# Attention and expert in units of 384 tokens, with other loads, load order and tile sets

## The chip, the cores and the metric

The kernel runs on one core of a Trainium2 chip, in one launch. The metric is the device time of the program in microseconds (us). A core has five engines that each run their own instructions in order: PE (TensorE, matmuls), DVE (VectorE), ACT (ScalarE), POOL (GpSimd) and SP (SyncE, which here only issues DMAs). They meet through semaphores. Matmuls write to PSUM, a small memory of eight banks per partition; a tile in it is free again when its readers are done.

## The reference

```python
# q, k, v: (4, 8, 768, 64) float32;  w_in: (512, 2048);  w_out: (2048, 512)
k_sum = k.reshape(B, H, nb, 32, D).max(axis=3)       # nb = 24 blocks of 32 tokens
v_sum = v.reshape(B, H, nb, 32, D).mean(axis=3)
scores_l = scale * q @ k.T, kept where |i - j| < 16, else -1e9
scores_s = scale * q @ k_sum.T + log(32)
a = softmax(concat(scores_l, scores_s))
x = a @ concat(v, v_sum)                             # then (tokens 3072, 512)
h = x @ w_in
out = (h * sigmoid(1.702 * h)) @ w_out               # (3072, 512) float32
```

A window attention with 24 block summaries beside the window feeds a two-layer expert whose activation is the quick form of gelu.

## The kernel before, in words

The work goes by batch: four batches of 768 tokens, 8 heads in 4 pairs p. For a batch the kernel loads q, k and v in float32, casts them to bf16, and turns each pair of k and q into the layout [head dimension, token] by transposes on PE (`tk`, line 237, and `tq`, line 266). From the transposed tile `ps_t` in PSUM, DVE copies k into `kx`: 12 tiles of 128 columns, each holding 64 tokens, the 24 block maxima and the 16 tokens on either side. `qz` holds q with zeros beside each head, so that one matmul makes the scores of both heads of a pair.

`vw` holds v in the same 12 tiles of rows, with a column of ones for the row sums. Its summary rows and its neighbours' rows are on other partitions than where they were made, so they are moved by six DMAs from SBUF to SBUF at the end of `vsum` (line 214): two of `vw<-vs` (the block sums) and four of `vw<-vw` (the halos). The matmuls of `values` read `vw` and wait for these six.

`scores` (276) makes 4 score tiles with one exponential on ACT and one multiplication by the mask on DVE; `values` (291) multiplies with `vw`, takes the reciprocal of the row sums and scales on DVE; `tx` (313) transposes the result into `xT`. `ff_in` (318) is the first layer with the gelu on ACT, written to `gT`; `ff_out` (328) the second, whose result ACT copies from `po` to `osb` and SP stores.

Every engine runs in the order in which the program is written: the class `_Ordered` records each instruction of `pe`, `dve`, `act`, `pool` and `sp` with that order (so all of them have line L27 in the profile). The order around the change is this. SP issues the loads of batch 0 (line 102), then, in `load_batch(1)`, those of batch 1, and then, in `vsum`, the six DMAs of `vw`. POOL issues the weights (`load_weights`, line 179, eight DMAs that also cast to bf16) after its casts of v. Attention of batch 0 then runs alone, as the list `att` says. From there the loop over batches (371) runs all of `ff_in` of batch b with the transposes of batch b+1 among them (the list `todo`), then all of `ff_out` of batch b with one piece of the attention of batch b+1 behind every four matmuls.

A load of q or k is one DMA for a head, with rows of 64 numbers (256 bytes): partition p takes tokens p, 128+p and so on. `kx`, `qz`, `vw` and `gT` exist once; the float32 tiles twice (`stage`, two buffers). PSUM has three buffers `sc` (transposes, scores, block sums), one `av` of two banks (values) and three `mm` (both expert layers).

Of the kernel before, what the change touches and what calls it, by code (L numbers as in the profile page):

```python
# [34 lines left out]
def kernel(  # L35
# [23 lines left out]
    HALF = S // 2  # L59

# [17 lines left out]
    def load_qk(b, p, which):  # L78
        src = q if which == "q" else k
        t = stage.tile([128, NJ, 2, D], F32, name=f"{which}f{p}", tag=f"{which}f{p}")  # L80
        for hh in range(2):
            sp.dma_start(out=t[:, :, hh, :],
                         in_=src[b, 2 * p + hh].rearrange("(j p) d -> p j d", p=128))
        return t

    def load_v(b):
        t = stage.tile([128, NJ, H, D], F32, name="vf", tag="vf")
        for hh in range(H):
            sp.dma_start(out=t[:, :, hh, :],
                         in_=v[b, hh].rearrange("(j p) d -> p j d", p=128))  # L90
        return t
# [3 lines left out]
    def load_batch(b):  # L95
        for p in range(NP):
            raw[b, "k", p] = load_qk(b, p, "k")
            raw[b, "q", p] = load_qk(b, p, "q")
            if p == 0:
                raw[b, "v"] = load_v(b)  # L100

    load_batch(0)


# [25 lines left out]
    for par, own, blk, halo in ((0, 0, 64, 96), (1, 64, 0, 32)):  # L130
        m = mk[:, par, :]
        nc.gpsimd.memset(m, 1.0)
        sel(mk[own:own + 64, par, :], window - 1, -1, 1)
        sel(mk[own:own + 64, par, :], window - 1, 1, -1)
        sel(mk[blk:blk + 32, par, :], nb - 1, 0, -1)
        hm = mk[halo:halo + 32, par, :]

        sel(hm, -(QT - 16 - (window - 1)), 1, -1)
        sel(hm, -16, 0, 1)
        lf = left[halo:halo + 32, :]  # L140

        nc.gpsimd.memset(lf, 1.0)
        sel(lf, window - 1 - 16, -1, 1)
        sel(lf, 15, 0, -1)
    for par, halo in ((0, 96), (1, 32)):
        sl = slice(halo, halo + 32)
        for t in range(2 + par, NQ, 2):
            nc.gpsimd.tensor_copy(out=mk[:, t, :], in_=mk[:, par, :])
        for t in range(par, NQ, 2):
            if t == NQ - 1:  # L150
                nc.gpsimd.tensor_copy(out=mk[sl, t, :], in_=left[sl, :])
            elif t > 0:
                nc.gpsimd.tensor_add(mk[sl, t, :], mk[sl, t, :], left[sl, :])


    kx, qz, xT = [], [], []
    for p in range(NP):
        kt = keep.tile([128, NQ, 128], BF16, name=f"kx{p}")
        k4 = kt.rearrange("p (j e) c -> p j e c", e=2)
        nc.vector.memset(k4[:, :, 0, 88:96], 0.0)  # L160
        nc.vector.memset(k4[:, :, 1, 24:32], 0.0)
        nc.vector.memset(kt[:, 0, 96:112], 0.0)
        nc.vector.memset(kt[:, NQ - 1, 48:64], 0.0)
        kx.append(kt)
        qt = keep.tile([128, NQ, 2, QT], BF16, name=f"qz{p}")
        nc.vector.memset(qt[0:64, :, 1, :], 0.0)
        nc.vector.memset(qt[64:128, :, 0, :], 0.0)
        qz.append(qt)
        xT.append(keep.tile([128, S], BF16, name=f"xT{p}"))
# [201 lines left out]
    for b in range(B):  # L371
# [23 lines left out]
        while todo:  # L395
            todo.pop(0)()
# [36 lines left out]
```

## Time and profile before

| | |
|---|---|
| times of 3 runs, us | 315.4, 315.85, 461.52 |
| median, us | 315.85 |
| the profiled execution: its time, us | 314.48 |
| its span from the first to the last instruction, us | 312.4 |
| busy in the span: PE, DVE, ACT, POOL, us | 222.7, 130.5, 121.1, 59.2 |
| mean granted TensorE clock | 0.861 |
| bytes moved by DMA, MB | 32.33, of it 27.88 on SP's queue |

The page of the profile gives, engine by engine, the busy share of the span in 40 equal slices of 7.8 us (one digit each, in tenths; 9 is 90% or more), with the granted TensorE clock and the load of the 16 DMA engines below. The chain of waits follows the work that ended last back to the start, each row with its start, its length and what it is. The groups list the instructions of one kind with count, busy time and the mean of one in ns, and the idle time of the engine before them with what ended it. "SPq" is SP's queue of DMA instructions. `po<-w_out_sb,gT` reads: the tile po is written from w_out_sb and gT.

### The profile page before, as it was taken

What the parts mean: (1) busy time and instruction counts of PE and PEld (TensorE: products, weight loads), DVE (VectorE), ACT (ScalarE), POOL (GpSimd) and SP (SyncE); (2) the same over time, 40 slices, a digit from 0 to 9 for tenths busy, and PEclk for the clock granted to TensorE, in tenths of its full rate; (3) what the DMA queues carried; (4) which work ended last, traced back from release to release, by engine and by line L of the source; (5) the groups of instructions that cost most, each with busy time, mean ns of one, the idle gap of its engine ahead of it and who ended that gap; (6) DMA issues with size and microseconds to landing.
All of it is one profiled execution on the core that took longest, in us unless ns stands there. A gap on an engine that the chain in (4) does not pass through costs nothing.

```text
span 312.4 us, 4176 instructions
## 1 busy us (share of the span) xinstructions
PE 222.7 (71%) x1578; PEld 135.5 (43%) x1592; DVE 130.5 (42%) x306; ACT 121.1 (39%) x218; POOL 59.2 (19%) x126
## 2 busy tenths in 40 slices
PE   1230000003565899999989999999999999999995
PEld 0110000003454466555556665555665555565442
DVE  6220010005887267366627736662872666100000
ACT  1340110000223365743366574327657342777111
POOL 7691000002002940000195000029200000000000
PEclk9985555555555699999999999999999999999999
DMA  9999999999990003111169981010040111100121
GB/s 172 217 197 195 195 196 224 219 201 214 210 200 0 0 3 61 28 52 51 67 149 207 220 154 69 34 67 36 0 85 4 69 48 53 37 0 2 47 87 67
DMA packets 85875, 32.33 MB, mean 103 GB/s; under 512 B 76128, under 2 KB 82784, under 8 KB 85856
## 3 DMA queue, kind: packets, MB, share of 16 engines
q1 hardware_dynamic: 81632, 27.88, 44.3%
q0 software_dynamic: 4224, 4.19, 8.0%
q8 instruction: 12, 0.20, 0.3%
q14 instruction: 7, 0.06, 0.1%
HBM read 27.26 MB, written 6.29 MB: 107 GB/s over the span
## 4 chain that ended last, share of the span: by engine, by line
PE 64%; SPq 21%; DVE 11%; issue 2%; DMA 1%; ACT 0%; ACTq 0%
PE ph L27 27%; PE po L27 25%; SPq L27 21%; DVE x_sb L27 5%; PE ps_t L27 4%; PE ps_av L27 4%; PE ps_s L27 3%; PE ps_vs L27 1%; DVE xT L27 1%; DVE kx L27 1%; DVE rc L27 1%; DVE qz L27 1%; DMA vw<-vw 1%; DVE a_sb L27 1%; DVE ks L27 1%
## 5 line engine op out<-in xcount | busy, mean ns | idle before, releaser
L27 PE MATMUL po<-w_out_sb,gT 128*128 128x512 bf16 x370 | 92.6, 379 | 0.7
L27 PE MATMUL ph<-xT,w_in_sb 128*128 128x384 bf16 x512 | 90.0, 329 | 0.5 <-DVE xT L27 0.5
L27 ACT ACTIVATE gT<-ph 128x384 bf16<-128x384 f32 x128 | 62.9, 491 | 38.1 <-PE ph L27 37.6
L27 PEld LDWEIGHTS <-w_in_sb 128*128 128x128 bf16 x512 | 49.3, 99 | 31.6 <-issue 2.5
L27 PE MATMUL ps_av<-vw,a_sb 128*128 128x130 bf16 x192 | 19.0, 243 | 57.0 <-DMA vw<-vw 53.6
L27 ACT ACTIVATE a_sb<-ps_s 128x512 bf16<-128x512 f32 x48 | 27.7, 595 | 80.8 <-PE ps_s L27 80.7
L27 PEld LDWEIGHTS <-gT 128*128 128x128 bf16 x384 | 34.6, 98 | 28.6
L27 POOL CAST vw<-vf 128x512 bf16<-128x512 f32 x42 | 24.0, 613 | 101.9 <-DMA out_dram<-osb 74.3
L27 PEld LDWEIGHTS <-a_sb 128*128 128x128 bf16 x192 | 15.2, 108 | 63.8 <-issue 53.7
L27 DVE TENSOR_TENSOR a_sb<-a_sb,mk 128x512 bf16<-128x512 bf16 x48 | 20.2, 425 | 45.4 <-ACT a_sb L27 45.0
L27 DVE TENSOR_TENSOR x_sb<-ps_av,rc 64x384 bf16<-64x384 f32 x64 | 35.5, 555 | 1.5
L27 ACT ACTIVATE osb<-po 128x512 f32<-128x512 f32 x24 | 14.3, 597 | 38.5 <-PE po L27 25.1
L27 PE MATMUL ps_s<-qz,kx 128*128 128x128 bf16 x192 | 20.1, 238 | 10.0 <-DVE qz L27 9.8
L27 DVE COPY kx<-ps_t 128x768 bf16<-128x768 bf16 (+2 forms) x48 | 15.2, 345 | 25.6 <-PE ps_t L27 25.5
L27 DVE RECIPROCAL rc<-ps_av 128x12 f32<-128x12 f32 x32 | 7.4, 231 | 41.9 <-PE ps_av L27 41.8
L27 PEld LDWEIGHTS <-kx 128*128 128x128 bf16 x192 | 15.8, 108 | 20.0 <-DVE qz L27 10.6
L27 POOL CAST kb<-kf 128x768 bf16<-128x768 f32 x12 | 9.9, 827 | 55.0 <-PE ps_t L27 54.2
L27 DVE COPY qz<-ps_t 64x768 bf16<-64x768 bf16 x32 | 17.6, 551 | 0.9 <-PE ps_t L27 0.7
L27 DVE TENSOR_REDUCE ks<-ps_t 128x24 bf16<-128x768 bf16 x16 | 15.2, 947 | 0.0
L27 PE MATMUL ps_t<-ident,x_sb 128*128 128x128 bf16 x96 | 10.6, 242 | 4.8 <-DVE x_sb L27 4.8
L27 PE MATMUL ps_t<-ident,kb 128*128 128x128 bf16 x96 | 9.3, 242 | 6.2 <-DVE kb L27 6.2
L27 ACT ACT_TABLE_LOAD x8 | 10.3, 1283 | 6.8 <-DMA qf<-in_q_dram 6.7
(40 smaller groups left out, 100.4 us busy)
## 6 DMA issues: line engine op xcount, KB each, us to landing
kf<-in_k_dram SPq DMA_DIRECT2D x32, 192.0 KB, 4.4
qf<-in_q_dram SPq DMA_DIRECT2D x32, 192.0 KB, 4.5
vf<-in_v_dram SPq DMA_DIRECT2D x32, 192.0 KB, 4.4
out_dram<-osb SPq DMA_DIRECT2D x24, 256.0 KB, 2.0
w_in_sb<-in_moe_w_in_dram POOLq DMA_DIRECT2D x4, 512.0 KB, 11.1
w_out_sb<-in_moe_w_out_dram POOLq DMA_DIRECT2D x4, 512.0 KB, 21.6
vw<-vs SPq DMA_DIRECT2D x8, 148.5 KB
vw<-vw SPq DMA_DIRECT2D x8, 99.0 KB, 3.9
```

The source lines that it names most:

```text
L27: r = f(*a, **kw)
```

## The change

The unit of the expert and of the attention is half a batch, 384 tokens: eight units u, with batch u // 2 and half u % 2. In a unit `ff_in` runs 16 groups of 4 matmuls, and `ff_out` 12 steps (3 tiles of 128 tokens by 4 parts), and beside the 12 steps stands the attention of the next unit, by the table `plan`. `scores` now makes 6 tiles in one go (one exponential and one mask multiplication of 768 columns). The k of a whole batch and its v are prepared in the `ff_in` of the unit with half 1 of the batch before, q half by half: `tq` for the second half in the `ff_in` of half 0, for the next batch's first half in that of half 1.

q and k are loaded with three consecutive tokens on a partition, a run of 768 bytes, two heads and 384 tokens to a DMA; v still in runs of 256 bytes, with 128 tokens of all heads to a DMA. Since the tokens now lie three to a partition, the transposes are plain matmuls with the identity as the moving side, float32 in PSUM, and each writes every third column (`p3[:, r]`). DVE therefore reads k and q in float32 from PSUM.

The order of the loads on SP is k of pairs 0 and 1, v, k of pairs 2 and 3, the first halves of q of pairs 0 and 1, the six DMAs of `vw`, the other q of batch 0, and then batch 1. POOL issues the weights behind its casts: the first chunk of `w_in` after the second cast of q, the other seven after the fourth.

`kx`, `vw` and `gT` exist twice (by batch or unit, even and odd), `qz` once for each half of a batch; the float32 tiles once. PSUM has two buffers `big` of two banks each (k and q transposes, scores, values), one `x` (block sums and `tx`), and three `mm` as before.

The core of the diff:

```diff
-    stage = ctx.enter_context(tc.tile_pool(name="stage", bufs=2))
+    stage = ctx.enter_context(tc.tile_pool(name="stage", bufs=1))
     castp = ctx.enter_context(tc.tile_pool(name="cast", bufs=3))
-    attp = ctx.enter_context(tc.tile_pool(name="att", bufs=2))
+    attp = ctx.enter_context(tc.tile_pool(name="att", bufs=4))
     outp = ctx.enter_context(tc.tile_pool(name="outp", bufs=3))
-    psc = ctx.enter_context(tc.tile_pool(name="psc", bufs=3, space=bass.MemoryType.PSUM))
-    pav = ctx.enter_context(tc.tile_pool(name="pav", bufs=1, space=bass.MemoryType.PSUM))
+    psb = ctx.enter_context(tc.tile_pool(name="psb", bufs=2, space=bass.MemoryType.PSUM))
+    psx = ctx.enter_context(tc.tile_pool(name="psx", bufs=1, space=bass.MemoryType.PSUM))
...
-    def load_qk(b, p, which):
-        src = q if which == "q" else k
-        t = stage.tile([128, NJ, 2, D], F32, name=f"{which}f{p}", tag=f"{which}f{p}")
-        for hh in range(2):
-            sp.dma_start(out=t[:, :, hh, :],
-                         in_=src[b, 2 * p + hh].rearrange("(j p) d -> p j d", p=128))
-        return t
+    def load_k(b, p):
+        t = stage.tile([128, 2, 2, JH, D], F32, name=f"kf{p}", tag=f"kf{p}")
+        for half in range(2):
+            sp.dma_start(out=t[:, half].rearrange("p h r d -> p h (r d)"),
+                         in_=k[b, 2 * p:2 * p + 2, half * HALF:(half + 1) * HALF]
+                         .rearrange("h (p r) d -> p h (r d)", r=JH))
+        raw["k", p] = t
...
+    def load_q(b, p, half):
+        t = stage.tile([128, 2, JH, D], F32, name=f"qf{p}{half}", tag=f"qf{p}{half}")
+        sp.dma_start(out=t.rearrange("p h r d -> p h (r d)"),
+                     in_=q[b, 2 * p:2 * p + 2, half * HALF:(half + 1) * HALF]
+                     .rearrange("h (p r) d -> p h (r d)", r=JH))
+        raw["q", p, half] = t
...
+    def load_v(b):
+        for c in range(3):
+            t = stage.tile([128, H, 2, D], F32, name=f"vf{c}", tag=f"vf{c}")
+            for j in range(2):
+                r0 = (2 * c + j) * 128
+                sp.dma_start(out=t[:, :, j, :],
+                             in_=v[b, :, r0:r0 + 128].rearrange("h p d -> p h d"))
+            raw["v", c] = t
...
+    kx = [[keep.tile([128, NQ, 128], BF16, name=f"kx{p}_{s}") for s in range(2)]
+          for p in range(NP)]
+    qz = [[keep.tile([128, TH, 2, QT], BF16, name=f"qz{p}_{s}") for s in range(2)]
+          for p in range(NP)]
+    vw = [keep.tile([128, NQ, H, VC], BF16, name=f"vw{s}") for s in range(2)]
+    vs = keep.tile([128, H, VC], BF16, name="vs")
+    xT = [keep.tile([128, HALF], BF16, name=f"xT{p}") for p in range(NP)]
+    gT = [keep.tile([128, NT, HALF], BF16, name=f"gT{s}") for s in range(2)]
...
+    def cast_k(eng, p):
+        t = castp.tile([128, 2, JH, 2, D], BF16, name="kb", tag="kb")
+        for half in range(2):
+            copy(eng, t[:, half].rearrange("p r h d -> p h r d"), raw["k", p][:, half])
+        cast["k", p] = t
...
+    def vrows(s):
+        w5 = vw[s].rearrange("p (j e) h c -> p j e h c", e=2)
+        dve.tensor_copy(out=vs[:, :, 0:D], in_=vs_ps[0].rearrange("p (h d) -> p h d", d=D))
+        sp.dma_start(out=w5[96:112, 1:NJ, 0], in_=w5[112:128, 0:NJ - 1, 1])
...
-        ps = trans(src.rearrange("p j h d -> p j (h d)"))
+        big = psb.tile([128, 1024], F32, name="ps_k", tag="big")
+        for half in range(2):
+            p3 = big[:, half * 512:half * 512 + HALF].rearrange("p (c r) -> p r c", r=JH)
+            for r in range(JH):
+                pe.matmul(out=p3[:, r], lhsT=src[:, half, r].rearrange("p h d -> p (h d)"),
+                          rhs=ident, start=True, stop=True)
+        copy(own, at(flat, 0, [[768, 2], [256, JH], [192, 2], [1, 64]]),
+             at(big, 0, [[512, 2], [128, JH], [64, 2], [1, 64]]))
+        dve.tensor_reduce(out=ks.rearrange("p (h n) -> p h n", h=2),
+                          in_=at(big, 0, [[512, 2], [block, nb // 2], [1, block]]),
+                          axis=AX.X, op=ALU.max)
...
+    def tq(p, half, e0, e1):
+        src = cast.pop(("q", p))
+        big = psb.tile([128, 1024], F32, name="ps_q", tag="big")
+        ps = big[:, 0:HALF]
+        p3 = ps.rearrange("p (c r) -> p r c", r=JH)
+        for r in range(JH):
+            pe.matmul(out=p3[:, r], lhsT=src[:, r].rearrange("p h d -> p (h d)"),
+                      rhs=ident, start=True, stop=True)
+        for hh, eng in ((0, e0), (1, e1)):
+            r = slice(hh * 64, hh * 64 + 64)
+            copy(eng, qz[p][half][r, :, hh, :], ps[r].rearrange("p (t c) -> p t c", c=QT))
...
+    def scores(b, half, p):
+        a_sb[p] = attp.tile([128, 2, TH, QT], BF16, name="a_sb", tag="a_sb")
+        a = a_sb[p]
+        big = psb.tile([128, 1024], F32, name="ps_s", tag="big")
+        ps = big[:, 0:2 * HALF].rearrange("p (t h c) -> p t h c", h=2, c=QT)
+        for i in range(TH):
+            pe.matmul(out=ps[:, i].rearrange("p h c -> p (h c)"),
+                      lhsT=kx[p][b % 2][:, half * TH + i, :],
+                      rhs=qz[p][half][:, i].rearrange("p h c -> p (h c)"),
+                      start=True, stop=True)
+        act.activation(out=a.rearrange("p h t c -> p t h c"), in_=ps,
+                       func=ACT.Exp, scale=scale)
...
+    load_k(0, 0)
+    load_k(0, 1)
+    load_v(0)
+    load_k(0, 2)
+    load_k(0, 3)
+    load_q(0, 0, 0)
+    load_q(0, 1, 0)
+    for p in range(NP):
+        clear_kx(dve, p, 0)
+    clear_vw(dve, 0)
+    dve.memset(vs[:, :, D:VC], float(block))
+    cast_k(dve, 0)
+    cast_k(act, 1)
+    tk(0, 0)
+    for p in range(NP):
+        clear_qz(pool, p, 0)
+    build_masks()
+    tk(1, 0)
+    for c in range(3):
+        for j in (2 * c, 2 * c + 1):
+            cast_v(act, 0, j, 0)
+            cast_v(pool, 0, j, 1)
+        vsum(0, (2 * c, 2 * c + 1))
+    vrows(0)
+    load_q(0, 2, 0)
+    load_q(0, 3, 0)
+    for p in range(NP):
+        load_q(0, p, 1)
+    cast_k(pool, 2)
+    cast_k(act, 3)
+    tk(2, 0)
+    tk(3, 0)
+    cast_q(pool, 0, 0)
+    tq(0, 0, act, act)
+    cast_q(pool, 1, 0)
+    load_w_in(0)
+    scores(0, 0, 0)
+    tq(1, 0, act, act)
+    cast_q(pool, 2, 0)
+    scores(0, 0, 1)
+    values(0, 0, 0)
+    tq(2, 0, act, act)
+    cast_q(pool, 3, 0)
+    scores(0, 0, 2)
+    values(0, 0, 1)
+    tx(0)
+    tq(3, 0, act, act)
+    scores(0, 0, 3)
+    values(0, 0, 2)
+    tx(1)
+    values(0, 0, 3)
+    tx(2)
+    tx(3)
+    for c in range(1, 4):
+        load_w_in(c)
+    for c in range(4):
+        load_w_out(c)
+    for p in range(NP):
+        clear_kx(pool, p, 1)
+        clear_qz(pool, p, 1)
+    clear_vw(pool, 1)
+    plan = {0: ["s0"], 1: ["s1"], 2: [], 3: ["v0"], 4: ["s2"], 5: ["v1"], 6: ["x0", "s3"],
+            7: ["v2"], 8: ["x1"], 9: ["v3"], 10: ["x2"], 11: ["x3"]}
...
+    for u in range(2 * B):
+        b, half = u // 2, u % 2
+        todo = {}
+        if half == 0:
+            for p in range(NP):
+                cast_q(pool, p, 1)
+                todo[3 + 3 * p] = [lambda p=p: tq(p, 1, dve, dve)]
+                if p == 2:
+                    todo[3 + 3 * p].append(lambda: None)
+        elif b + 1 < B:
+            s = (b + 1) % 2
+            todo = {1: [lambda: tk(0, s)], 2: [lambda: tk(1, s)],
+                    4: [lambda: vsum(s, (0, 1, 2))],
+                    5: [lambda: vsum(s, (3, 4, 5)), lambda: vrows(s)],
+                    6: [lambda: tk(2, s)], 8: [lambda: tk(3, s)],
+                    9: [lambda: tq(0, 0, dve, dve)], 11: [lambda: tq(1, 0, dve, dve)],
+                    12: [lambda: tq(2, 0, dve, dve)], 14: [lambda: tq(3, 0, dve, dve)]}
+            cast_k(pool, 0)
+            cast_k(pool, 1)
+            for j in range(NJ):
+                cast_v(pool, s, j, 0)
+                cast_v(pool, s, j, 1)
+            cast_k(pool, 2)
+            cast_q(pool, 0, 0)
+        for nt in range(NT):
+            ff_in(u, nt)
+            if half == 1 and b + 1 < B:
+                if nt == 2:
+                    cast_k(pool, 3)
+                if nt == 9:
+                    cast_q(pool, 1, 0)
+                    cast_q(pool, 2, 0)
+                if nt == 11:
+                    cast_q(pool, 3, 0)
+            for f in todo.get(nt, ()):
+                f()
+        if half == 0 and b + 1 < B:
+            pass
+        nxt = u + 1 < 2 * B
+        i = 0
+        order = ([(ms, part) for part in range(4) for ms in range(JH)] if u == 0 else
+                 [(ms, part) for ms in range(JH) for part in range(4)])
+        for ms, part in order:
+            ff_out(u, ms, part)
+            if nxt:
+                beside((u + 1) // 2, (u + 1) % 2, i)
+            i += 1
+            if half == 0 and b + 1 < B and i == 1:
+                load_k(b + 1, 0)
+                load_k(b + 1, 1)
+                load_v(b + 1)
+                load_k(b + 1, 2)
+                load_k(b + 1, 3)
+                for p in range(NP):
+                    load_q(b + 1, p, 0)
+                for p in range(NP):
+                    load_q(b + 1, p, 1)
```

The order of the instructions shows three places. The first is SP at the start of the program. Before (`vf`, `kf`, `qf` are the float32 tiles of v, k and q; those with numbers of 258 and more are batch 1's):

```order
L27 DMA kf_258<-in_k_dram 128x6x64 x2
L27 DMA qf_261<-in_q_dram 128x6x64 x2
L27 DMA vf<-in_v_dram 128x6x64 x8
L27 DMA kf_273<-in_k_dram 128x6x64 x2
L27 DMA qf_276<-in_q_dram 128x6x64 x2
L27 DMA kf_279<-in_k_dram 128x6x64 x2
L27 DMA qf_282<-in_q_dram 128x6x64 x2
L27 DMA kf_285<-in_k_dram 128x6x64 x2
L27 DMA qf_288<-in_q_dram 128x6x64 x2
L27 DMA vw<-vs 24x6x528 x2
L27 DMA vw<-vw 16x5x528
L27 DMA vw<-vw 16x6x528 x2
```

After (`kf_139` and `kf_142` are k of pairs 2 and 3 of batch 0, `vw_113` is the first of the two sets of `vw`):

```order
L27 DMA kf_139<-in_k_dram 128x2x192 x2
L27 DMA kf_142<-in_k_dram 128x2x192 x2
L27 DMA qf_145<-in_q_dram 128x2x192
L27 DMA qf_147<-in_q_dram 128x2x192
L27 DMA vw_113<-vw_113 16x5x528
L27 DMA vw_113<-vw_113 16x6x528 x2
L27 DMA vw_113<-vw_113 16x5x528
L27 DMA vw_113<-vs 24x6x528 x2
L27 DMA qf_266<-in_q_dram 128x2x192
L27 DMA qf_268<-in_q_dram 128x2x192
```

All 24 loads of batch 1 stood ahead of the six DMAs of `vw`; now these stand behind two of the q tiles of batch 0 and ahead of the other six, and batch 1 comes later still.

The second is POOL where it issues the weights. Before, behind the last work on the masks:

```order
L151 COPY mk<-left 32x64
L27 CAST vw<-vf 128x8x64 x6
L27 DMA w_in_sb<-in_moe_w_in_dram 128x4x512 x4
L27 DMA w_out_sb<-in_moe_w_out_dram 128x4x512 x4
L27 CAST kb<-kf_258 128x768
```

After (`qf_266` and `qf_268` are the first halves of q of pairs 2 and 3):

```order
L27 DMA w_in_sb<-in_moe_w_in_dram 128x4x512
L27 CAST qb<-qf_266 128x2x3x64
L27 CAST qb<-qf_268 128x2x3x64
L27 DMA w_in_sb<-in_moe_w_in_dram 128x4x512 x3
L27 DMA w_out_sb<-in_moe_w_out_dram 128x4x512 x4
```

Seven of the eight weight DMAs now stand behind two casts that need loads which SP issues after the six DMAs of `vw`.

The third is DVE in the preparation of the next batch, beside `ff_in`. Before, for pair 3 (`kx_196`, `qz_201`):

```order
L27 COPY kx_196<-ps_t 128x6x2x64
L27 TENSOR_REDUCE ks<-ps_t 128x24
L27 COPY kx_196<-ps_t 128x5x2x16
L27 COPY kx_196<-ps_t 128x6x2x16
L27 COPY kx_196<-ks 128x6x2x24
L27 COPY qz_201<-ps_t 64x12x64 x2
```

After (`kx_1_104` is the second set of `kx` of pair 3, `qz_0_105` to `qz_0_109` the first halves of q of pairs 0 to 2):

```order
L27 CAST kx_1_104<-ps_k 128x2x2x2x16
L27 CAST kx_1_104<-ps_k 128x2x16
L27 CAST kx_1_104<-ps_k 128x6x2x16
L27 COPY kx_1_104<-ks 128x6x2x24
L27 CAST qz_0_105<-ps_q 64x6x64 x2
L27 CAST qz_0_107<-ps_q 64x6x64 x2
L27 CAST qz_0_109<-ps_q 64x6x64 x2
```

The copies from `ps_k` and `ps_q` are casts (float32 to bf16), there is one more of them for a pair (six instructions of DVE for k where five stood), and q's four pairs follow all of k instead of standing each behind its own k.

More of the change, by code (lines that the diff above doesn't have):

```diff
@@ L86, in load_v @@
-    def load_v(b):
[L87 to L91, printed above, removed]
-    raw = {}
[L95 to L102, printed above, removed]
+    raw = {}
@@ L145 @@
[L145 to L169, printed above, removed]
@@ L203, with copy @@
-    vw5 = vw.rearrange("p (j e) h c -> p j e h c", e=2)
-    def cast_v(b, par, first):
-        src = raw[b, "v"]
-        dst = vw5[:, :, par, :, 0:D]
-        for j in range(NJ):
-            if first and j % 2 == 0:
-                act.activation(out=dst[:, j], in_=src[:, j], func=ACT.Copy)
-            else:
-                pool.tensor_copy(out=dst[:, j], in_=src[:, j])
-    def vsum():
-        ps = psc.tile([128, H * D], F32, name="ps_vs", tag="sc")
-        for j in range(NJ):
+    def copy(eng, out, in_):
+        if eng is act:
+            act.activation(out=out, in_=in_, func=ACT.Copy)
+        else:
+            eng.tensor_copy(out=out, in_=in_)
@@ new lines, with beside @@
+    scores(0, 0, 3)
[14 more added lines that the diff above has]
+            7: ["v2"], 8: ["x1"], 9: ["v3"], 10: ["x2"], 11: ["x3"]}
+    def beside(b, half, slot):
+        for what in plan[slot]:
+            p = int(what[1])
+            if what[0] == "s":
+                scores(b, half, p)
+            elif what[0] == "v":
+                values(b, half, p)
+            else:
+                tx(p)
```

257 lines of the change are left out of this document (103 added, 154 removed), and 4 rows, old and new, of the table att.

## The prediction

> **What bounds the kernel now.** I read the page first, for where PE is idle.
>
> ```profile
> span 312.4 us, 4176 instructions
> PE   1230000003565899999989999999999999999995
> PEclk9985555555555699999999999999999999999999
> DMA  9999999999990003111169981010040111100121
> ```
>
> PE is nearly idle for 13 of 40 slices (7.8 us each) and full from there. In the idle part the DMA engines are full and the granted clock falls to half. So there are two stages with different limits. The waits and the chain say what ends the first.
>
> ```profile
> PE ps_av L27 <- DMA vw<-vw: 53.6, 1, 53.6
> ```
> ```profile
> 69.17 2.89 DMA vw<-vw
> 73.04 0.24 DVE rc L27
> 73.31 0.55 DVE x_sb L27
> 73.87 0.56 DVE x_sb L27
> 74.44 0.56 DVE kx L27
> 75.00 0.87 DVE ks L27
> 75.86 0.32 DVE kx L27 x2
> 76.21 0.23 DVE kx L27
> 76.44 0.46 DVE qz L27
> 76.92 0.57 DVE qz L27
> 77.53 0.62 PE ps_s L27 x4
> 104.02 7.71 PE ph L27 x40
> 118.26 1.29 PE ps_vs L27 x6
> 119.56 1.30 PE ph L27 x8
> ```
>
> The first `values` waits 53.6 us, until 72.06, for the halo rows of `vw`, which stand on SP behind batch 1. Then batch 0's attention runs alone, mostly on DVE, to 104.0. The first 40 matmuls of `ff_in` take 7.71 us where five times 1.30 would be 6.5: the clock comes back, for 1.2 us. From 104.0 PE sets the pace:
>
> ```profile
> 130.86 0.22 PE ps_s L27 x4
> 134.12 0.34 PE ps_av L27 x6
> 134.47 0.86 PE po L27 x4
> 139.80 0.34 PE ps_t L27 x6
> ```
> ```profile
> 156.58 0.52 PE L27 MATMUL ps_av<-vw,a_sb 128*128 128x130 bf16 x6 [0.62 <-DVE x_sb L27]
> 158.58 0.34 PE L27 MATMUL ps_t<-ident,x_sb 128*128 128x128 bf16 x3 [0.45 <-DVE x_sb L27]
> 159.57 6.17 PE L27 MATMUL ph<-xT,w_in_sb 128*128 128x384 bf16 x37 [0.16 <-DVE xT L27]
> ```
>
> PE's only waits here are 1.2 us (0.62 + 0.45 + 0.16) at the end of a batch, three times. A group of four `ph` is 0.65 us, a step of four `po` 0.86.
>
> **The start, part by part.** The loads and the casts of batch 0:
>
> ```profile
> 5.56 0.59 DVE L27 CAST kb<-kf 128x768 bf16<-128x768 f32 x1
> 14.04 3.23 ACT L27 ACTIVATE vw<-vf 128x512 bf16<-128x512 f32 x6 [5.25 <-DMA vf<-in_v_dram]
> 14.20 3.40 POOL L27 CAST vw<-vf 128x512 bf16<-128x512 f32 x6 [2.15 <-issue]
> 18.31 3.14 POOL L27 DMA_DIRECT2D w_in_sb<-in_moe_w_in_dram  x4 [0.72 <-issue]
> 63.33 1.70 SPq L27 DMA_DIRECT2D qf<-in_q_dram  x2
> ```
> ```profile
> 51.00:65.00 14.00, 0.00 (x0) 0.00 (x0) 0.00 (x0) 0.00 (x0) 0.00 (x0) 0.50 1.22 219
> ```
> ```profile
> q0 software_dynamic: 4073, 4.04, 85.1%
> ```
>
> The second row is a window without engine work; its last figure is 219 GB/s for 256-byte runs alone. The third covers 22 to 50 us: the weights' 4.04 MB written are 8.1 MB read, so 289 GB/s or more beside SP's loads.
>
> The first twelve loads (2.36 MB) had landed at 14.0. In the change the first ten DMAs are as many bytes (k of two pairs, v), so v is there by 14 at the latest, and in three pieces, so that its casts run as it lands. The next k (0.79 MB) takes 2.7 us at the weights' rate and 3.6 at 219: no row has 768-byte runs, these are the bounds, and I take 16. POOL casts its half of v by 16.5 (3.4 us, the last piece landing near 13.5) and k of pair 2 by 17.3.
>
> The six DMAs of `vw` now wait only for the casts and the sums of v. They go out from 16.5 to 20.5 and land after the 2.89 us of the first row of the chain: 23.4. **That removes the 53.6 us wait**; what is late next is k, through DVE:
>
> ```profile
> L27 DVE COPY kx<-ps_t 128x768 bf16<-128x768 bf16 x16 | 8.9, 557 | 25.6 <-PE ps_t L27 25.5
> L27 DVE CAST vs<-ps_vs 128x512 bf16<-128x512 f32 x4 | 2.8, 692 | 8.7 <-PE ps_vs L27 8.7
> L27 DVE TENSOR_TENSOR a_sb<-a_sb,mk 128x512 bf16<-128x512 bf16 x48 | 20.2, 425 | 45.4 <-ACT a_sb L27 45.0
> L27 DVE TENSOR_TENSOR x_sb<-ps_av,rc 64x384 bf16<-64x384 f32 x64 | 35.5, 555 | 1.5
> L27 ACT ACTIVATE a_sb<-ps_s 128x512 bf16<-128x512 f32 x48 | 27.7, 595 | 80.8 <-PE ps_s L27 80.7
> L27 ACT ACTIVATE gT<-ph 128x384 bf16<-128x384 f32 x128 | 62.9, 491 | 38.1 <-PE ph L27 37.6
> L27 ACT ACT_TABLE_LOAD x8 | 10.3, 1283 | 6.8 <-DMA qf<-in_q_dram 6.7
> ```
>
> From float32 in PSUM DVE needs 555 ns for 384 columns and 692 for 512, so 0.97 us for 768, where the bf16 copy took 0.56 (the lower bound). In the chain a pair's k steps on DVE took 1.98 us (74.44 to 76.44); with 0.41 for the cast and some 0.15 for one instruction more, 2.55. Pair 2 then holds DVE from 18.2 to 20.7 and pair 3 to 23.3.
>
> From here the two PSUM tiles `big` set the order: scores of pair p need the tile that `values` of pair p-2 gave back, that is, its `x_sb`. An exponential of 768 columns is 0.80 us (491 and 595 ns at 384 and 512), a pair's two copies of q on ACT 1.0 (two of 384 columns), scores of six tiles at half clock 0.9 (four took 0.62), the mask 0.6 (425 ns for 512), rc and both x_sb 1.35. So: scores 0 at 23.0, exponential to 24.7, copies of q of pair 1, scores 1, exponential to 27.3, mask, and `x_sb` of pair 0 done at 29.3. Each further pair costs scores, exponential, mask and x_sb: 3.6 us, so 36.5 after two. Then one copy to `xT`, the last rc and x_sb, another copy, the last transposes and their copy, 2.8 us: **`ff_in` starts at 39.3; I take 39.5 against 104.0, -64.5.** Bounds: 34.5, if loads and POOL are 2 us sooner, PE keeps its full clock (2 us) and the casts cost as bf16; 46, if each of four pairs takes 1 us more and POOL's masks hold v back by 2.5.
>
> Do the weights keep up? Seven of eight chunks leave POOL between 24.5 and 30 (0.77 us each) and come at worst one in 3.5 us, the last at 49; batch 1's and q's small runs beside them (2 MB, 9 us) make it 58. PE needs the last of `w_out` at 62. So they cost nothing, with 4 us of cover.
>
> The Trainium skill ("DMA: Bandwidth & Descriptors", Specifications) says that transfers of 512 bytes and more run at line rate, smaller ones not. By it the two k loads of 0.79 MB would take under 2 us each, an estimate from its 16 times 27 GiB/s, and the sum would be some 2 us less. No row of the profile has such runs.
>
> **The steady part.** Matmuls of every kind are as many as before, on as many columns. The transposes write every third float32 column: `ps_s` (float32, 0.22 for four) and `ps_t` (bf16, 0.34 for six) cost the same 0.056 a matmul, so the type costs nothing; the stride is in no row. I take 0; twice the time on 156 transposes would be 8.7 us. The other terms:
>
> - Batch 0's second half of attention moves behind 39.5: 24 scores 1.3, 24 values 1.4, 12 transposes of x 0.7 and 12 of q 0.7: **+4.1**.
> - In units 1, 3 and 5 the k of the next batch and half of q stand beside `ff_in`. PE has 16 groups (10.4), k and q transposes (2.0) and block sums (1.3), 13.7 us; DVE has four times 2.55, the sums' cast 0.6 and four times 1.03 for q (the rows at 76.44 and 76.92; half the columns, float32): 14.9. DVE is the slower, and the two `big` tiles make PE wait: q of pair 0 is due at 9.1, its tile is free at 9.8; q of pair 1 due at 11.3, free at 12.4; q of pair 2 at 13.2 and 13.7. 2.3 us, three times: **+6.8** (0 with bf16 prices, 13.5 if DVE takes a fifth longer). Before, k and q took turns in three one-bank tiles and DVE needed 3.0 for a pair in 3.3 us of PE.
> - At the end of a unit DVE's last x_sb now has two steps of `po` (1.7 us) and a transpose over it, and needs 1.35 plus one copy: the waits of 1.2 go, **-3.7**.
> - ACT changes its table twice in each unit instead of twice in each batch. After the last `po` it copies 512 columns (0.60), loads (1.28) and makes the first gelu (0.49), 2.37 us; PE has three `mm` tiles, 1.95 us of groups, over it. So some 0.4 at each of 7 seams, against 0.15 at four (the 37 `ph` above took 6.17 for 6.02): **+2.2**. The cover gone, a seam costs the load's 1.3.
>
> The ramp of 1.2 us and the tail after the last `po` stay. The sum on the profiled execution is 314.48 - 64.5 + 4.1 + 6.8 - 3.7 + 2.2 = 259.4; the median shown stands 1.4 higher, so **260.8 us**.
>
> **The rivals.**
>
> *More waits on the two PSUM tiles.* Scores, values, k and q all pass through them, in `ff_out` too. If DVE is a fifth slower (POOL casts beside it) the odd units lose 2.2 us more each and the seven seams 0.6: 272. For it: DVE's 14.9 against 13.7. Against: in `ff_out` DVE has 9.1 us of work in 13.8 (four masks, rc, x_sb and xT).
>
> *Batch 1 late.* If 768-byte runs bring nothing, the DMA work that before ended near 69 (SP's last load of batch 1 left at 64) ends near 75, since the engines idle while `vw` waits. v of batch 1 is wanted at 69.5 in unit 1; if POOL and the rest fall behind it by 7 us: 268. Against: v comes 2.36 MB before the end.
>
> *A better start and no waits of DVE.* 34.5 and 0 for the odd units: 249.
>
> *Slower: the clock.* If the short waits in the odd units make the granted clock fall to 0.5, as it stood from 22 to 101 us, and it stays down in these units, each of three has 27.5 us of PE work to do at half speed, +82: 343. It decides from 55 us of such work on. Against: two gaps of 0.62 and 0.45 us within 2.5 us (156 to 159) left the row PEclk at 9. The Trainium skill ("TensorE: Matmul & The Clock Gate", The HAM clock gate) lets the clock fall only after an idle window of about 3.4 us, which speaks against it; its section on psum-queue depth-cycling tells of short idles that do the same, which speaks for it. The rows here bear out the first.
>
> **How the numbers follow.** Chances: forecast 0.62, more waits 0.14, batch 1 late 0.11, better start 0.10, slower 0.03. The range takes the bounds of the start (-5 to +6.5), of the odd units (-6.8 to +6.7) and part of the stride's 8.7: 247 to 278, which holds all cases but the slow one and the far ends of the others. Faster by over 2%, about what a measurement of this kernel can tell from no change, is 0.96; within 2% 0.01; slower 0.03.
>
> **What would show it.** Right: the wait of `ps_av` for `vw` is gone or under 5 us; the first `ph` starts between 35 and 46; in the odd units PE's `ps_q` waits for DVE about 2 us in all; a group of `ph` stays at 0.65 and PEclk at 9 after the start; a unit takes 24 to 29 us; k casts near 0.97 us. Wrong: `ph` or `po` waiting for weights, PE waiting in `ff_out`, six `ps_k` over 0.34, a clock of 5 behind unit 0.

## The result and the profile after

| | before | after |
|---|---|---|
| median of 4 runs, us | 315.69 | 264.65 |
| lowest to highest, us | 315.4 to 461.52 | 264.14 to 265.18 |
| the profiled execution, us | 314.48 | 264.85 |
| its span, us | 312.4 | 263.1 |

The ratio is 0.8386 [0.8363, 0.8409]: 51.0 us less, 3.9 us above the forecast. One run of before, 461.52, is far from the other three; the ratio leaves it out.

The page of the profile after, the rows that answer to those of before; a slice is now 6.6 us:

```profile
span 263.1 us, 4275 instructions
PE   2543749999998999999989999999989999999994
PEclk9998555999999999999999999999999999999999
DMA  6969999998432118993150129972130210011012
```

PE is full from the seventh slice on: the idle start has gone from 13 slices of 7.8 us to 6 of 6.6. The chain of waits, with the start of a piece, its length and what it is, in the part that answers to the wait for `vw`:

```profile
14.23 2.79 POOL vw L27 x5
17.02 0.91 POOL kb L27 x2
20.28 0.80 SPq L27
21.12 6.46 DMA qf<-in_q_dram
30.08 0.80 PE ps_s L27 x6
32.61 0.48 ACT qz L27
33.11 0.49 ACT qz L27
33.65 0.81 PE ps_s L27 x6
39.31 0.48 PE ps_x L27 x3
39.79 5.10 PE ph L27 x16
```

No landing of a `vw` DMA is on it. SP issues the first of the six at 16.49 and the others behind the cast that ends at 17.02, about as forecast, and the first `values` waited for none of them. What the chain does hold is SP itself, which is busy issuing the six until 21.08 and only then issues the load of q of pair 2, which lands at 27.58. These rows of SP's and PE's timelines show when the six leave and that `values` does not wait:

```profile
16.49 2.73 SPq L27 DMA_DIRECT2D vw<-vw  x4
19.32 1.75 SPq L27 DMA_DIRECT2D vw<-vs  x2
```
```profile
23.11 0.49 PE L27 MATMUL ps_s<-qz,kx 128*128 128x128 bf16 x6 [1.07 <-ACT qz L27]
27.28 0.81 PE L27 MATMUL ps_av<-vw,a_sb 128*128 128x130 bf16 x6
```

The first scores start at 23.1 (23.0 was forecast), the pairs follow in 3.6 us (30.08 to 33.65; 3.6), and the first `ph` is at 39.8 (39.5). What each of the four scores waits for last is ACT, with its two copies of q:

```profile
PE ps_s L27 <- ACT qz L27: 4.3, 4, 1.1
```

Behind the start, in the third stage of the program (unit 1, `ff_in` beside the k of batch 1), the chain shows what the forecast had at nothing:

```profile
69.31 0.66 PE ps_k L27 x6
75.16 0.67 PE ps_k L27 x6
75.86 0.96 DVE kx L27
80.81 0.49 PE ps_q L27 x3
```

Six transposes of k cost 0.66 us of PE, where six before cost 0.34 (the row `ps_t` of the prediction). The waits of PE from 39.6 on (total, times, longest) and, for comparison, of before from 104 on:

```profile
PE ps_q L27 <- DVE kx L27: 2.2, 3, 0.7
PE ps_x L27 <- DVE xT L27: 1.2, 6, 0.2
PE ph L27 <- ACT gT L27: 0.7, 4, 0.2
```
```profile
PE ps_av L27 <- DVE x_sb L27: 1.9, 3, 0.6
PE ps_t L27 <- DVE x_sb L27: 1.4, 3, 0.5
PE ph L27 <- DVE xT L27: 0.5, 3, 0.2
```

4.1 us against 3.8: the steady part waits about as long as it did. No row of `ph` or `po` waits for weights.

### The profile page after: what moved, and what is told of

Its sections match the earlier page's. It is cut to its first block, busy times and chain, and to the rows that moved or that the text cites. A ratio compares the mean times of both kernels' runs of the same rounds, so it can differ in the third digit from the quotient of the medians.

```text
span 263.1 us, 4275 instructions
## 1 busy us (share of the span) xinstructions
PE 234.2 (89%) x1571; PEld 142.0 (54%) x1592; DVE 146.7 (56%) x336; ACT 131.3 (50%) x218; POOL 75.5 (29%) x185
## 4 chain that ended last, share of the span: by engine, by line
PE 74%; DVE 8%; POOL 6%; ACT 5%; DMA 2%; issue 2%; SPq 1%; ACTq 0%; POOLq 0%
PE po L27 29%; PE ph L27 26%; PE ps_s L27 4%; PE ps_q L27 4%; PE ps_av L27 4%; DVE kx L27 4%; PE ps_x L27 3%; DMA qf<-in_q_dram 2%; PE ps_k L27 2%; DVE ks L27 2%; ACT L27 2%; DVE x_sb L27 2%; PE ps_vs L27 1%; POOL qz L27 1%; POOL vw L27 1%
## 5 line engine op out<-in xcount | busy, mean ns | idle before, releaser
L27 PE MATMUL ph<-xT,w_in_sb 128*128 128x384 bf16 x512 | 97.7, 335 | 0.7 <-ACT gT L27 0.7
L27 DVE CAST qz<-ps_q 64x384 bf16<-64x384 f32 x56 | 31.1, 555 | 28.6 <-PE ps_q L27 28.0
L27 POOL CAST qb<-qf 128x384 bf16<-128x384 f32 x32 | 16.1, 513 | 101.5 <-PE ps_q L27 63.6
L27 DVE TENSOR_TENSOR a_sb<-a_sb,mk 128x768 bf16<-128x768 bf16 x32 | 18.4, 575 | 33.8 <-ACT a_sb L27 32.9
L27 ACT ACTIVATE a_sb<-ps_s 128x768 bf16<-128x768 f32 x32 | 25.2, 809 | 23.4 <-PE ps_s L27 23.3
L27 DVE CAST kx<-ps_k 128x768 bf16<-128x768 f32 (+1 forms) x64 | 25.5, 439 | 10.3 <-PE ps_k L27 10.3
L27 PE MATMUL ps_k<-ident,kb 128*128 128x128 bf16 x96 | 15.5, 351 | 7.6 <-DVE kb L27 3.9
L27 POOL CAST kb<-kf 128x384 bf16<-128x384 f32 x26 | 13.5, 542 | 29.2 <-PE ps_k L27 26.5
L27 PE MATMUL ps_q<-ident,qb 128*128 128x128 bf16 x96 | 16.7, 316 | 4.6 <-DVE kx L27 3.4
L27 PEld LDWEIGHTS <-kx 128*128 128x128 bf16 x192 | 13.9, 102 | 10.4 <-issue 4.1
L27 PEld LDWEIGHTS <-kb 128*128 128x128 bf16 x96 | 11.2, 139 | 11.8 <-POOL kb L27 4.4
```

Source lines behind the costliest of these rows:

```text
L27: r = f(*a, **kw)
```

## The experiments

The theory is that the order of the transfers at the start makes the gain, that half units bring the start further forward, and that the 768-byte runs bring nothing and cost time on PE (the strided transposes) and on DVE (float32). The rivals: the gain comes from the long runs, or from the half units and double tiles alone.

**1. One line of before moved** (`x1_order`).

```diff
     load_weights()
-    load_batch(1)
     vsum()
+    load_batch(1)
```

> The kernel before with one line moved: load_batch(1) stands behind vsum(), so that SP issues the six DMAs of vw ahead of batch 1's 24 loads. All else is as before (whole batches, 256-byte runs, single sets). Theory (the order on SP held the start): the 53.6 us wait of the first values for vw falls to some 5 to 10, since the rows land near 24; the attention of batch 0 alone took 31 us from its first values to the first matmul of the expert, so that matmul comes at 55 to 60 instead of 104, and the time is 268 to 273. Rival (the DMA work of 17.8 MB held the start, whatever its order): the first expert matmul waits for batch 1 or weights until about 72 or later, and the time is 283 or more. Second rival (the units of 384 tokens brought most of the 51 us): the wait only moves to the attention, and the time stays over 300.

Measured: 288.17 us (286.2 to 290.33), ratio 0.9101 [0.9038, 0.9163]. The sign held, the size did not: it is the rival's number. SP's timeline, the chain, and the wait of `values`:

```profile
21.58 7.42 SPq L27 DMA_DIRECT2D vw<-vs  x2
29.05 3.45 SPq L27 DMA_DIRECT2D vw<-vw  x4
```
```profile
31.90 14.01 DMA vw<-vw
```
```profile
PE ps_av L27 <- DMA vw<-vw: 27.3, 1, 27.3
```

The six no longer stand behind the loads of batch 1, yet the last of them, issued at 31.9, lands 14.0 us later, where the last one of before took 2.89. The weights (POOL issues them from 18.35 on) hold the 16 DMA engines meanwhile: from 32 to 46 us the packets of their queue take 80.4% of the engines' time. The order among the queues has to change too, not only that on SP.

**2. Before, with the weights behind the rows as well** (`x5_order_w`, then `x10_order_w2`).

```diff
-    load_weights()
-    load_batch(1)
     vsum()
     for p in range(1, NP):
         cast_qk(0, p, "k", True)
-        cast_qk(0, p, "q", True)
+        cast_qk(0, p, "q", p < NP - 1)
+    load_weights()
+    load_batch(1)
```

> The kernel before with two moves: batch 1's loads behind the six DMAs of vw (as in the run with the order alone), and the eight weight DMAs on POOL behind a cast of q of pair 3, which POOL now makes instead of ACT, so that they leave only when all loads of batch 0 have landed. All else is as before. Theory (order on two queues is the gain: in the run with SP's order alone the rows of vw still took 14 us to land among the weights, and the first values came at 46): batch 0's 4.7 MB land by about 24, the rows of vw by 26, the first expert matmul comes 31 to 32 us after, at 57 to 59, time 267 to 272. Rival (without the units of 384 tokens batch 1 or the weights are late for the first layer): the first expert matmul comes as early, but the first layer or its transposes wait, time 276 or more.

Measured: 281.89 us (281.83 to 282.1), ratio 0.892 [0.8888, 0.8952]; again the rival's side. The first part of the theory held in kind: the rows land in 4.36 us instead of 14, and the first `ph` is at 61.50, 2.5 later than expected. But PE waits for `vw` twice, the second time for batch 1:

```profile
24.97 4.36 DMA vw<-vw
95.32 3.43 DMA vw<-vw
```
```profile
91.47 1.79 SPq L27 DMA_DIRECT2D vw<-vs  x2
93.31 2.60 SPq L27 DMA_DIRECT2D vw<-vw  x4
```
```profile
98.95 0.81 PE L27 MATMUL ps_av<-vw,a_sb 128*128 128x130 bf16 x6 [6.08 <-DMA vw<-vw]
```

With the start earlier, `load_batch(b + 2)`, which stands ahead of batch 1's `vsum`, still waits for its buffers when the rows of batch 1 are due: the same fault as in before, one batch later. So the second kernel also moves these loads back:

```diff
-            if nt == 6 and b + 2 < B:
+            if nt == 9 and b + 2 < B:
                 load_batch(b + 2)
```

> The run with whole batches and the order on two queues, with one more move: the loads of batch 2 (and of batch 3) stand behind the DMAs of vw of the batch before them (issued at nt 9 of the first layer instead of nt 6). Theory (in the run without this the same fault came back one batch later: 24 loads of batch 2 ahead of the rows of vw of batch 1, for 10.8 us of wait): that wait goes, the rest stays, first expert matmul at 61 to 62, time 269 to 272. Rival (POOL's casts of batch 1 are late as well): a wait of 5 us or more stays, time 276 or more.

Measured: 272.89 us (272.5 to 272.97), ratio 0.8621 [0.8594, 0.8647], 0.9 above the range. It is 9.0 us below x5, of which the wait that went is 6.1. Most of the other 2.9 stands right behind that wait, where PE runs at about half its rate. These are the first four `po` behind batch 1's first `values`, in x5 and in x10:

```profile
99.55 1.91 PE L27 MATMUL po<-w_out_sb,gT 128*128 128x512 bf16 x4
```
```profile
92.76 1.02 PE L27 MATMUL po<-w_out_sb,gT 128*128 128x512 bf16 x4
```

From that `values` to the `po` behind the next `values`, x5 takes 5.26 us (98.95 to 104.21) and x10 2.64 (92.41 to 95.05) for the same matmuls: 2.6 of the 2.9. (The longest of x5's two waits, 10.8 us, is that of batch 0 at 29.47, which stays, at 11.5.) The chain of x10:

```profile
25.49 4.28 DMA vw<-vw
62.10 8.07 PE ph L27 x40
```

Three moves in the old kernel, with whole batches, runs of 256 bytes and single sets of tiles, give 43 of the 51 us. The rival that only half units or long runs make the gain falls. The first `ph` of the change is another 22.3 us earlier than x10's, but its total is only 8.2 below: the table of terms further down has what the change pays behind its start.

**3. The six DMAs of `vw` late again, in the changed kernel** (`x6_late_vw`): ten loads of batch 1 ahead of them on SP.

```diff
+    load_k(1, 0)
+    load_k(1, 1)
+    load_v(1)
     vrows(0)
```

(Their later issue is taken out.)

> The changed kernel with one part undone: k of pairs 0 and 1 and v of batch 1 (2.36 MB) stand on SP ahead of the six DMAs of vw. Theory (the start hangs on the place of these six): at 219 GB/s the bytes ahead take some 11 us, the first values come at 33 to 37 instead of 27.3, the first expert matmul at 46 to 50, time 271 to 275. Rival (the start hangs on DVE and the two PSUM tiles, the rows of vw have slack): the first expert matmul within 3 us of 39.6, time under 268.

Measured: 270.36 us (269.41 to 271.23), ratio 0.8553 [0.8521, 0.8584]. The first `ph` is at 46.43 and `values` waits 5.6 us for `vw<-vs`, as expected; the time is 0.6 below the range. Half units do not protect against this order.

**4. All weights early, in the changed kernel** (`x7_early_w`).

```diff
+    for c in range(4):
+        load_w_in(c)
+    for c in range(4):
+        load_w_out(c)
     vrows(0)
```

(The later issues of the weights are taken out.)

> The changed kernel with one part undone: all eight weight DMAs stand on POOL right behind the casts of v, ahead of the casts of k of pair 2 and of q. Theory (weights ahead of the small transfers stretch these): the rows of vw and the last q land at 35 to 46, the first expert matmul comes at 52 to 60, time 277 to 285. Rival (only POOL's 6 us of issuing stand in the way of its casts): the first expert matmul at 45 to 47, time 269 to 272.

Measured: 270.84 us (270.09 to 270.97), ratio 0.8564 [0.8536, 0.8591]. My theory of a long wait for `vw` falls; the rival's numbers stand, with the first `ph` at 46.36. POOL's timeline:

```profile
16.97 3.14 POOL L27 DMA_DIRECT2D w_in_sb<-in_moe_w_in_dram  x4
20.07 3.00 POOL L27 DMA_DIRECT2D w_out_sb<-in_moe_w_out_dram  x4
23.00 1.02 POOL L27 CAST kb<-kf 128x384 bf16<-128x384 f32 x2
```

The cast of k of pair 2 starts 6.0 us later than in the change (17.0), because POOL is busy issuing eight DMAs for 6.1 us. The rows left SP at 16.48 to 21.4, beside the first weights, and the first `values`, now at 33.68, did not wait for them. So the place of the weights matters twice: for the small transfers that leave behind them, as in x1, and for what POOL itself has to do next.

**5. The stride alone** (`x2_contig`): the transposes write their 128 columns side by side. The tokens of a tile then stand in another order than the reference has them; the instructions are as many, on as many columns.

```diff
-            p3 = big[:, half * 512:half * 512 + HALF].rearrange("p (c r) -> p r c", r=JH)
+            p3 = big[:, half * 512:half * 512 + HALF].rearrange("p (r c) -> p r c", r=JH)
...
-        p3 = ps.rearrange("p (c r) -> p r c", r=JH)
+        p3 = ps.rearrange("p (r c) -> p r c", r=JH)
```

> The changed kernel with one edit: the transposes of k and q write 128 columns side by side in PSUM instead of every third one. The tokens of q and k then stand in another order, so this computes another attention; every instruction has the same count and size. Theory (the stride of 12 bytes doubles the time of a transpose on PE): six ps_k take 0.34 us instead of 0.66 and three ps_q 0.17 instead of 0.33. That is 2.6 us less in the four units with half 0. In units 1, 3 and 5 DVE is then the slower one again, as the prediction worked out (16.0 us for their first layer, where 16.9 were measured), 0.9 us less each. In all some 5 us less than the changed kernel: 259 to 260.5. Rival (float32 output or the plain matmul with the identity costs the time, not the stride): ps_k stays at 0.66 and the time at 264.5.

Measured: 258.93 us (258.51 to 259.58), ratio 0.8178 [0.8141, 0.8215]: 5.7 below the change and 0.1 below the range. The chain and PE's waits from 39.4 on:

```profile
39.49 5.12 PE ph L27 x16
68.75 0.35 PE ps_k L27 x6
82.46 0.17 PE ps_q L27 x3
```
```profile
PE ps_q L27 <- DVE kx L27: 4.3, 6, 0.9
PE ps_q L27 <- DVE qz L27: 0.6, 3, 0.2
```

Six `ps_k` are 0.35 instead of 0.66, three `ps_q` 0.17 instead of 0.33. With 12 groups of k and 28 of q behind the first `ph`, that is 3.7 + 4.5 = 8.2 us of PE. PE now waits 4.9 us for DVE in these units instead of 2.2, so 2.7 come back: 5.5 of the 5.7.

**6. Short runs** (`x3_256`): q and k loaded with 256-byte runs as before, a head to a DMA, transposes side by side, still float32, and the tokens in the reference's order.

```diff
-            sp.dma_start(out=t[:, half].rearrange("p h r d -> p h (r d)"),
-                         in_=k[b, 2 * p:2 * p + 2, half * HALF:(half + 1) * HALF]
-                         .rearrange("h (p r) d -> p h (r d)", r=JH))
+            sp.dma_start(out=t[:, hh],
+                         in_=k[b, 2 * p + hh].rearrange("(j p) d -> p j d", p=128))
```

> The changed kernel with q and k loaded in runs of 256 bytes again (token p, 128+p and so on to partition p; the DMAs go by head, so q takes twice as many), which also lets the transposes write columns side by side; float32 in PSUM as in the change. The result is the reference's. Theory (the 768-byte runs bring the start little, since POOL and DVE set it, and PE pays for them): PE as in the run with columns side by side, the first expert matmul within 1.5 us of 39.6, time 259 to 262. Rival (longer runs are what makes the loads early enough): k of pairs 2 and 3 and batch 1's v land late, the first expert matmul at 43 or later or waits in unit 1, time 265 to 270.

Measured: 258.65 us (258.13 to 259.46), ratio 0.8168 [0.8122, 0.8213], 0.3 below the range; x2 had 258.93 on the same chip. The first `ph` is at 39.36, x2's at 39.49. The 768-byte runs bring no time here.

The Trainium skill ("DMA: Bandwidth & Descriptors", Specifications) asks for 512 bytes and more for line rate. The runs do not refute it for a load by itself, but no time of this kernel hangs on it. The one load on the chain of the start, q of pair 2, is late because SP issues it behind the six DMAs of `vw`; POOL casts it at 27.64 in the change and at 27.78 in x3.

**7. Short runs and bf16 transposes** (`x4_256_bf16`): x3 with `pe.transpose` into bf16 tiles.

```diff
-        big = psb.tile([128, 1024], F32, name="ps_k", tag="big")
+        big = psb.tile([128, 2048], BF16, name="ps_k", tag="big")
...
-                pe.matmul(out=p3[:, r], lhsT=src[:, half, r].rearrange("p h d -> p (h d)"),
-                          rhs=ident, start=True, stop=True)
+                pe.transpose(out=p3[:, r], in_=src[:, half, r].rearrange("p h d -> p (h d)"),
+                             identity=ident)
```

> As the run with 256-byte runs, and the transposes of k and q are in bf16 in PSUM as before the change, so that DVE copies bf16. The result is the reference's. Theory (after the stride, the odd units hang on DVE's float32 reads through two PSUM tiles): DVE needs about 2.1 us for a pair's k instead of 2.55 and 0.7 for a pair's q instead of 1.0, PE's waits for ps_q in units 1, 3 and 5 go, their first layer takes 13.8 to 14.2 us, time 252 to 256. Rival (the waits come from the number of tiles, not from DVE's speed): the waits stay at 1 to 2 us a unit and the time within 1.5 us of the run with float32.

Measured: **253.11 us** (252.14 to 253.77), ratio 0.799 [0.795, 0.8029], the fastest version here. Groups of DVE in the change, then in x4 (busy time, mean ns of one, idle before):

```profile
L27 DVE CAST kx<-ps_k 128x768 bf16<-128x768 f32 x16 | 15.3, 953 | 10.3 <-PE ps_k L27 10.3
L27 DVE CAST qz<-ps_q 64x384 bf16<-64x384 f32 x56 | 31.1, 555 | 28.6 <-PE ps_q L27 28.0
```
```profile
L27 DVE COPY kx<-ps_k 128x768 bf16<-128x768 bf16 x16 | 8.9, 555 | 9.5 <-PE ps_k L27 9.5
L27 DVE COPY qz<-ps_q 64x384 bf16<-64x384 bf16 x56 | 19.8, 354 | 32.3 <-PE ps_q L27 31.8
```

The copy of k falls from 953 to 555 ns, and from 39.2 on PE waits for neither k nor q: x3's 4.9 us (as in x2) are gone, of 5.5 between the medians.

The Trainium skill ("VectorE: DVE Perf Modes", Why PSUM operands drop a tier) gives an operand in PSUM the base rate in float32 and at most twice that in bf16. These rows agree: 1.7 times for 768 columns.

**8. A better start, tried twice** (`x8_start`, `x9_start2`): x4 with q of pairs 2 and 3 loaded ahead of the rows of `vw`, and the q transposes of the start in `mm` tiles; x9 also casts one q more on POOL ahead of the last seven weight DMAs.

```diff
-    load_q(0, 0, 0)
-    load_q(0, 1, 0)
+    for p in range(NP):
+        load_q(0, p, 0)
...
+        if e0 is act:
+            big = pmm.tile([128, 1024], BF16, name="ps_q", tag="mm")
```

In x9, besides:

```diff
     tx(3)
+    cast_q(pool, 0, 1)
     for c in range(1, 4):
         load_w_in(c)
```

> The run with 256-byte runs and bf16 transposes, with two more edits for the start: the transposes of q of the first unit take tiles of the mm buffers, which are idle then, so that the two big tiles serve scores and values alone; and the first halves of q of pairs 2 and 3 are loaded ahead of the rows of vw. The result is the reference's. Theory (in the start each pair of heads cost 3.6 us because scores, exponential, mask and x_sb followed one another through the two tiles): a pair costs 2.3 to 2.8 us, the first expert matmul comes at 35.5 to 37.5 instead of 39.3, time 249 to 251.5. Rival (ACT or POOL sets the pace of the start): no earlier than 38.5, time 252 to 254.

> The run with the two edits for the start, with one more: the cast of the second half of q of pair 0, whose load SP issues behind the rows of vw, stands on POOL ahead of the last seven weight DMAs, so that these leave after the rows have landed. The result is the reference's. Theory (in the run before, q two places earlier let the casts of q end 7 us sooner, and with them the weights start at 21.5 beside the rows of vw, which then took 9 us to land): the rows land near 25, the first values come at 25 to 26.5 instead of 31.8, the first expert matmul at 36 to 38, time 249 to 251.5. Rival (the rows are slow for another reason, such as the q loads beside them): the first values still near 31, time 255 to 257.

Measured: 256.26 us (255.3 to 257.3), ratio 0.8111 [0.8084, 0.8137], and 255.82 us (254.14 to 256.87), ratio 0.8082 [0.8054, 0.811]. Both are slower than x4, with the first `ph` at 43.28 and 41.15 instead of 39.29; both expectations missed. The waits of x4, x8 and x9 in this order:

```profile
PE ps_av L27 <- DMA vw<-vs: 0.7, 1, 0.7
```
```profile
PE ps_av L27 <- DMA vw<-vs: 8.0, 1, 8.0
```
```profile
PE ps_av L27 <- DMA vw<-vs: 5.8, 1, 5.8
```

In x8, earlier q makes POOL finish its casts sooner, so seven chunks of weights leave at 21.53 instead of 29.08, beside the rows, whose last DMA then lands after 9.06 us. x9 holds the weights back until 30.59, and the last one still takes 7.06. In both, the rows also leave 2.2 us later (18.5 to 23.2 instead of 16.4 to 21.1), because four more q loads stand ahead of them on SP. What slows them in x9, the q loads beside them or the one chunk of `w_in` at 19.87, stays open: x4 has a chunk at 20.14 and q loads behind the rows too.

The two runs also answer the other half of the theory. With the q transposes out of the two `big` tiles a pair still takes 3.16 us (in x8 the scores of pairs 2 and 3 start at 33.98 and 37.14), where x4 takes 3.24 (29.91 to 33.15) and 2.3 to 2.8 were expected. So sharing the tiles with q is not what sets the pace of the pairs.

## Why the prediction came out right, point by point

The forecast for the profiled execution was 259.4; it took 264.85. Term by term, in us:

| term | forecast | measured |
|---|---|---|
| start, to the first `ph` | -64.5 | -64.2 (104.02 to 39.79) |
| half of batch 0's attention moved | +4.1 | not apart; taken as +4.1 |
| stride of the transposes | 0 | +8.2 (x2) |
| PE's waits in units 1, 3, 5 | +6.8 | +2.2 |
| ends of batches and units | -3.7 | -2.6 (3.8 to 1.2) |
| seams of the table loads | +2.2 | +0.7 |
| the clock's return | 0 | +1.3 |
| outside the span | 0 | -0.3 (2.08 to 1.75) |
| sum | -55.1 | -50.6, of -49.6 in all |

- **The start** was right in its cause, in its sum and in its first part: the rows leave at 16.5, the first scores start at 23.1. Two steps behind that were not as forecast. The rows were to land at 23.4, 2.89 us after the last issue; in the trace their last packet ends at 26.2, and in x4, with the same order of these DMAs, `values` waits until 25.98 for a row issued at 20.33. So about 1 us of cover is left in the change, not 4. And a pair takes 3.6 us, but not by scores, exponential, mask and `x_sb` one after the other through the two tiles. The pieces of the chain from 30.08 to 33.65 are scores 0.80, values 0.65, a transpose of x 0.32, transposes of q 0.74 and ACT's copies of q 0.97; the scores of pair 3 start at 33.65, before the last `x_sb` of pair 1 ends at 33.74. That both sums come to 3.6 is luck. The experiments show the cause of the gain. With the rows late again the first `ph` goes back to 46.4 (x6), and the old kernel with a new order comes to 62.1 (x10). The 22.3 us from there to 39.8 come with the half units and the rest of the change, which no run takes apart; of these, x3 rules out the long runs.
- **The stride** is the term that was mis-sized. The prediction wrote that it is in no row, took 0 and gave 8.7 as the bound; it is 8.2, nearly the bound. Six `ps_k` over 0.34 was one of its signs of being wrong, and it came. The reasoning that the type costs nothing was right (0.35 for six in float32, 0.34 in bf16), and said nothing on the stride. The Trainium skill ("PSUM — Partial Sum Buffer", Specifications (TRN2)) says that any non-contiguous access pattern slows matmuls significantly; it gives no factor, the rows of k here give 1.9. I had weighed two other rules and not this one, which speaks against the change.
- **PE's waits in the odd units** were too large by 4.6, and the two errors are one: a slower PE (by 8.2 us over all units, about 1.9 in each odd one) gives DVE time to catch up. x2, without the stride, shows 4.9 of the 6.8 us. Together the two terms were forecast at 6.8 and came to 10.4.
- **Ends and seams**: the `x_sb` waits went, as forecast; a transpose of x waits up to 0.2 for `xT` in their place. The seams are hidden better than the 0.4 each that I took.
- **The clock's return**: 16 `ph` take 5.10 where four times 0.65 is 2.6, so 2.5 instead of 1.2. The prediction took it as unchanged. It is no constant: in x9 the first 16 take 3.80.
- **The rivals**: more waits on the `big` tiles did not come, neither in `ff_out` nor elsewhere. Batch 1 was not late, with runs of 768 bytes or of 256. The fall of the clock in the odd units did not come either: PE's waits there are 0.7 us at most and the groups of `ph` keep 0.65. A wait of 6.08 us, in x5, did slow PE behind it, by 2.6 us. 1.0 us of the sum stays unassigned.

The time lies in the upper half of the range: 264.65 is 3.9 above the forecast, and the stride alone is more than that. The shorter waits in the odd units took back 4.6 of it, which the forecast had not foreseen.

## What to carry to other kernels

A small transfer that the next stage waits for has to be placed on every queue at once: on its own, where it must not stand behind prefetches that wait for buffers, and against the others, where megabytes issued just ahead make it take 14 us instead of 3. A layout that makes the runs of a load longer can be paid for at its other end: here the long runs gave nothing and the strided writes with float32 reads cost 11.5 us (264.65 to 253.11). After an order is repaired, look for the same fault one stage later, because the next prefetch stands in the same place.

## What the runs showed of the hardware

- A matmul of 128 columns that writes every third float32 column of PSUM holds PE for 0.110 us (0.66 for six); side by side it is 0.058 (0.35), and in bf16 0.057 (0.34 in x4).
- A small DMA from SBUF to SBUF lands after 2.89 us in before, where the weights are long in place, after 14.01 beside them (x1), and after 4.36 where they are issued behind it (x5).
- A wait of 6.08 us of PE is followed by matmuls at about half rate: four `po` take 1.91 us instead of 1.02, twice, and the page's row PEclk of x5 has a 5 in that slice. Behind PE's waits of 0.7 us and less in the change the groups keep their 0.65.
- The granted clock of the records does not tell how fast PE is at the start. This is the page's row of x4, where the profile after has fives, and its chain:

```profile
PEclk9999999999999999999999999999999999999999
```
```profile
39.29 5.09 PE ph L27 x16
```

The first 16 `ph` take 5.09 us at a recorded clock of 9 (x4) and 5.10 at one of 5 (the change). Of the runs of the change, 264.85 us had a mean clock of 0.961 and 265.18 us one of 1.0. So the prediction's rival on the clock was argued from a row that does not decide it; the durations of equal groups do.
